# The row maximum of attention scores in two reductions, and new order tables, in a transformer block on one NeuronCore

## The chip, the cores and the metric

The kernel runs on one core of a Trainium2 chip. The metric is the device time of one execution in microseconds; the kernel before took 999.41 us as the median of three runs (999.37 to 1000.24). All data are float32. TensorE (PE) multiplies, VectorE (DVE), ScalarE (ACT) and GpSimd (POOL) work on its results, SyncE (SP) issues most of the DMAs. PE writes its products into PSUM banks of 128 partitions by 512 float32 numbers.

## The reference

One block with adaptive layer norms: sliding-window attention with 32 heads of 20, then an MLP applied to each token. There are 2048 tokens of width 640, a window of 256, and an MLP width of 1536.

```python
mod = (_silu(c) @ w_mod).reshape(c.shape[0], 6, 1, -1)
sa, ca, ga, sb, cb, gb = (mod[:, 0], ..., mod[:, 5])
h = _layernorm(x) * (1 + ca) + sa
x = x + ga * _A_ref(h, A_wqkv, A_wo)      # q, k, v; scores * 20 ** -0.5 with
                                          # 0 <= i - j < 256; softmax; @ v; @ wo
h = _layernorm(x) * (1 + cb) + sb
x = x + gb * _B_ref(h, B_w1, B_b1, B_w2, B_b2)   # layernorm, @ w1 + b1, gelu, @ w2 + b2
```

## The kernel before, in words

**Precision.** Each large product is made three times, of operands split into a high and a low part: `hhi x whi`, `hlo x whi` and `hhi x wlo`. The low parts are made by DVE or POOL (`hlo`, `wlo`, `stage`), as tables say (`LOV`, `LOWP`, `HIA`).

**Stages.** In the start (until 48.8 us of the profile), the first 1024 tokens are normalized, the modulation is worked out from `c`, and the first columns of q and k are projected, in an order written out by hand (`ORDER`, after `RUN0` warm-up products that only keep PE at work). Attention follows, to 556.5 us, then its tail to 596.9 us, then the MLP, in four blocks of 512 tokens.

**The attention loop** (`for t in range(n + LAG + PVLAG + 4)`, lines 1302 to 1351) has 128 score items: two halves of the tokens, eight quads of four heads, eight blocks of 128 queries. Item `t` computes its scores twice. First they are computed with queries on the partitions, for the row maxima only (`s_batch`, the tile `s`). Eleven iterations later (`LAG`), they come with keys on the partitions (`e_batch`, the tile `e`), with the negated maximum fed in through two more rows of the operand. An iteration does, in this order on PE: the products of `e` for item t − 11 and of `s` for item t, interleaved (`score_batch`); the products of the probabilities with v of an earlier item (`pv_stage`, tile `o`); then products that a plan puts there (`plan[t, h]`) as filling: projections of later columns (`pp`, with `pp_late` and `ppo` of the same kind), transposes (`psx`, `pv`, `pm`, `xt`, `yt`), the attention's output product (`wo`), and the sums that spread a modulation vector over all rows (`pmr`). How many `pp` products an iteration gets is set by `EXTRA`, one number for each `t`; where other steps land is set by further tables. On DVE an iteration does the mask of `e`, the mask of `s`, the maximum of `s` over the keys (`s_max`, the tile `nm`) and then planned steps: statistics of layer norms, low parts, sums. ACT takes the exp (`pt`), copies `o` out (`oT`), and makes high parts. In every eighth iteration of the first half (t = 18, 26, 34, 42, ...) there is no `e` item, so PE has only `s` products, and the filling.

**Banks.** Of `s` and `e` there is one buffer each. From t = 11 on, the 4 heads of `s` (384 keys each) share 3 banks: in slots 0 to 3, at columns 0, 384, 768 and 1152, so that slots 0 and 1 lie in banks 0 and 1, slots 2 and 3 in banks 1 and 2. Two heads are multiplied in one half of the array's rows, the other two in the other, side by side. The next products of `s` can start when the reduction of the item before has read the tile. Those of `e` can start when its exp has. The order of the products in a batch is a list:

```python
ONE = "0a 0d 0b 0e 0c 0f".split()
BOTH = ['0f', '0c', '0d', '1a', '1b', '1d', '0b', '1e', '0a', '0e', '1c', '1f']
```

The digit says whether it is of the first (`e`) or second (`s`) of the batch; with `ONE` there is only one of the two. The letters a, b and c are products of slots 0 and 1 (a in bank 1, b and c in bank 0), d, e and f those of slots 3 and 2 (d and e in bank 2, f in bank 1).

**The tail** (t from 128 on, the first iterations at 556.5 us) has no `s` any more: `e`, `o`, the output products `wo` of the fourth block of tokens, its second layer norm (`sta`, `xb`, `y`, `stb`), and its transposes `yt`, which the MLP's first products need. `WARM` puts warm-up products at places of it, `CROSS` says how much of this block's work falls into the tail, `SUMS_LAST` in which iterations ACT takes the exp before it copies `o`.

Every instruction is recorded through a helper, so all stand at line 119 in the profile of before (121 in the changed kernel), and are told apart by the names of their tiles.

Of the kernel before, what the change touches and what calls it, by code (L numbers as in the profile page):

```python
# [9 lines left out]
F32 = mybir.dt.float32  # L10
# [3 lines left out]
ALU = mybir.AluOpType  # L14
AX = mybir.AxisListType
PSUM = bass.MemoryType.PSUM

P = 128
# [14 lines left out]
RUN0 = 37  # L33
# [4 lines left out]
ORDER = ('T00 M1 L00 S0 S1 S2 R3 S3 T01 R12 L01 P00 N M2 T02 P01 M3 R3 T03 T10 L03 L02 T11 M4 R1 C L10 P02 T04 R6 P10 L11 T12 L04 P03 L12 T13 L13 P11 P04 E0 T14 Y00 P12 P13 L14 Y01 P14')  # L38
LOWP = ['L10', 'L03', 'L00', 'L14', 'L13', 'L12']


UNITS = ((0, 'q1', 'k1', 'v0', 'v1', 'q2', 'k2', 'v2', 'q3', 'k3', 'v30', 'q40', 'k40', 'v40', 'k41', 'q41', 'v41', 'v31'), (1, 'q10', 'k00', 'k10', 'q00', 'q01', 'k01', 'q11', 'k11', 'v1', 'v0', 'q2', 'k2', 'k3', 'q3', 'v2', 'v3', 'q4', 'k4', 'v4'))
FAST = 10
LNS = [-11.0, -3.5, -1.25, -1.5, 1.25, -1.0, -0.25]
LOV = [0, 1, 3, 4, 5, 6, 7, 12, 14, 17, 18, 19, 21, 23, 25, 26, 29, 40, 41, 42, 43, 46, 49, 50, 53, 56, 58, 60]
HIA = [0, 2, 6, 7, 9]
MV = [9, 12, 15, 19, 20, 21, 23, 26, 27]
# [4 lines left out]
V_COST = 2.84  # L52
# [5 lines left out]
EXTRA = {9: -2, 10: -4, 11: 7, 12: 1, 13: -2, 14: -2, 16: -2, 18: -3, 20: -5, 21: 4, 22: 6, 23: 3, 24: 1, 25: 4, 26: -1, 27: 5, 28: -4, 29: 3, 30: -3, 31: -3, 33: 4, 34: -3, 35: 2, 36: 3, 37: 3, 38: -6, 40: -2, 41: -5, 42: -3, 44: -7, 46: 2, 50: 1, 51: 1, 52: -8, 53: 7, 54: -10, 55: 1, 56: -6, 57: 3, 59: 8, 60: -2, 61: -1, 63: -1, 64: -1, 65: 2, 66: -8, 67: -2, 68: -2, 69: -2, 70: -1, 71: 3, 72: 6, 73: 3, 75: -1, 76: -2, 77: -3, 78: -2, 79: -3, 80: -3, 81: -9, 82: 19, 83: 6, 84: -2, 85: -1, 86: 2, 88: 3, 90: 2, 91: 1, 92: 3, 93: -6, 94: -11, 96: 8, 97: 1, 98: -1, 99: 5, 101: 3, 102: 1, 103: 6, 104: -4, 105: -2, 106: -1, 107: -2, 108: 3, 110: 3, 111: 6, 112: -1, 114: -1}  # L58

EARLY = {3: (5, 0, 0), 5: (3, 0, 0), 6: (3, 0, 0), 7: (3, 0, 0), 9: (5, 0, 0), 12: (1, 0, 0), 13: (0, 0, 0), 14: (0, 0, 0), 15: (5, 0, 0), 16: (5, 0, 0), 17: (4, 0, 0), 19: (4, 0, 0), 24: (4, 0, 0), 30: (5, 0, 0), 32: (0, 0, 0), 33: (3, 0, 0), 35: (5, 0, 0), 37: (5, 0, 0), 39: (5, 0, 0), 40: (4, 0, 0), 41: (3, 0, 0), 42: (4, 0, 0), 43: (2, 0, 0), 44: (2, 0, 0), 45: (0, 0, 0), 47: (5, 0, 0)}  # L60

AFTER = {0: 1, 2: 2, 3: 2, 4: 3, 5: 1, 6: 1, 7: 1, 9: 1, 10: 2, 11: 1, 12: 2, 14: 1, 15: 1, 19: 1, 20: 1, 22: 1, 23: 2, 25: 1, 32: 1, 35: 1, 36: 3, 38: 3, 40: 1, 41: 3, 42: 2, 43: 3}

SUMS_LAST = [13, 14, 18, 25, 31, 42, 46, 50, 52, 55, 58, 60, 61, 62, 63, 64, 75, 76, 77, 78, 79, 88, 90, 91, 95, 99, 101, 103, 108, 109, 110, 111, 115, 116, 117, 120, 122, 126, 127, 131, 132, 133, 136, 139]
LEAST = 4
MOST = 10
MODS = [[10.0, 17.0], [17.75, 27.5], [69.5, 79.25]]
WOS = [88.5, 91.75, 98.75, 110.25, 112.0, 113.25, 116.0]
W1S = [115.0, 122.0, 133.75]
RS = [[81.75, 82.5], [82.5, 88.75]]  # L70
TOMID = 110
WARM = {(130, 1): 3}
LATE_AT = [110.25, 110.5, 110.75, 111.5, 113.75, 114.0, 116.5]
TAIL0 = [115.25, 120.25, 124.25, 129.0]
NEXT = 134.0
CROSS = 0.72
LO0 = 4.6
PER = 4.821
LATE = 0.8152
TAIL_AT = {'rd': -1.372, 'ri': -1.024, 'load': -0.924, 'om': -0.246, 'oh': 0.058, 'ol': 0.133, 'w00': 0.287, 'w01': 0.36, 'w02': 0.382, 'w03': 0.416, 'w04': 0.511, 'add0': 0.569, 'sa0': 0.649, 'w10': 0.71, 'w11': 0.711, 'w12': 0.722, 'w13': 0.855, 'w14': 0.865, 'add1': 0.885, 'sa1': 1.178, 'n1': 1.2, 'm0': 1.327, 'x0': 1.343, 'x1': 1.544, 'm1': 1.344, 'sb0': 1.505, 'sb1': 1.557, 'n2': 1.683, 'y0': 1.844, 'y0l': 1.922, 'y1': 2.026, 'y1l': 2.38}  # L80
# [44 lines left out]
def block_kernel(ctx: ExitStack, tc: tile.TileContext, x, wqkv, wo, w1, b1, w2, b2, c, crow, wmod, wcol, sel, outT):  # L125
# [425 lines left out]
    def score_batch(batches):  # L551
# [51 lines left out]
    def s_max(it, s, c0):  # L603
# [3 lines left out]
        nc.vector.tensor_reduce(it["quad"]["nm"][:, :, it["key"][2]], s[:, :, max(c0, P) : 384], AX.X, ALU.max)  # L607
# [878 lines left out]
```

## Time and profile before

| what | us |
|---|---|
| median of 3 runs (lowest, highest) | 999.41 (999.37, 1000.24) |
| the profiled execution | 1000.15 |
| its span, from the first instruction to the last | 998.4 |
| PE, DVE, ACT, POOL busy | 955.0, 593.0, 443.1, 479.4 |
| mean granted clock of PE, as a share of full speed | 0.988 |
| the stages' ends: start, attention, tail, MLP | 48.8, 556.5, 596.9, 985.0 |

A row of the profile gives line, engine, operation, tiles (out<-in), shapes, how often, then the busy time in us and the mean of one in ns, then the idle time ahead and the instruction whose end ended it. A timeline row gives start and duration in us, the instruction, how many follow each other (a matmul of full float32 shows as two records), and in brackets the idle time ahead with the releaser. The iteration numbers `t` are counted from the `s` batches.

### The profile page before, as it was taken

Reading aid. Unit: us, or ns where it says so; the run is one execution under the profiler, and the core shown is the slowest. Engines: PE = TensorE matmul, PEld = TensorE weight load, DVE = VectorE, ACT = ScalarE, POOL = GpSimd, SP = SyncE. Lnnn points to the kernel's source line nnn. Section 1 sums busy time; section 2 is a strip of 40 time slices with the busy share of each in tenths; the row PEclk is TensorE's granted clock in tenths of the full one; section 3 lists DMA queues with packets and bytes.
Section 4 is the critical chain, followed back from the end, with each engine's and each line's share of the span. In section 5 each row is a group of like instructions: output and inputs, shape, how many; then the busy total and the mean of one; then the engine's idle time right before and its main releaser. Section 6 shows DMA issues by size and latency. Waiting matters only on the chain.

```text
span 998.4 us, 19991 instructions
## 1 busy us (share of the span) xinstructions
PE 955.0 (96%) x7745; PEld 753.3 (75%) x7745; DVE 593.0 (59%) x938; ACT 443.1 (44%) x777; POOL 479.4 (48%) x671
## 2 busy tenths in 40 slices
PE   8899999999999999999998879999999999999997
PEld 8777677666777777777676667888888888888886
DVE  6664868878766787767678656565444443333112
ACT  3724545566655544554445664333432343333122
POOL 4324555576764254544536855654543444442221
PEclk9999999999999999999699999999999999999999
DMA  8364877637768368834672235344422344124113
GB/s 301 105 217 140 273 241 257 195 106 211 227 198 254 91 198 258 245 110 152 198 190 64 78 95 188 125 122 137 135 85 85 103 126 123 41 66 145 53 44 115
DMA packets 98974, 152.17 MB, mean 152 GB/s; under 512 B 8864, under 2 KB 42112, under 8 KB 98880
## 3 DMA queue, kind: packets, MB, share of 16 engines
q1 hardware_dynamic: 89664, 142.50, 46.9%
q10 hardware_dynamic: 9216, 8.39, 2.7%
q8 instruction: 62, 1.02, 0.4%
q14 instruction: 32, 0.26, 0.1%
HBM read 98.51 MB, written 51.58 MB: 150 GB/s over the span
## 4 chain that ended last, share of the span: by engine, by line
PE 78%; DVE 10%; ACT 5%; issue 3%; POOL 2%; DMA 2%; DVEq 0%; ACTq 0%; POOLq 0%
PE pp L119 16%; PE out L119 16%; PE h L119 15%; PE e L119 7%; PE o L119 6%; PE wo L119 6%; PE s L119 5%; DVE e L119 4%; ACT pt L119 3%; DVE nm L119 2%; PE ppo L119 2%; PE warm L119 1%; DVE s L119 1%; PE yt L119 1%; DMA w2r<-in_w 1%
## 5 line engine op out<-in xcount | busy, mean ns | idle before, releaser
L119 POOL TENSOR_SCALAR_AFFINE_SELECT pt<-pt 128x512 f32<-128x512 f32 x192 | 129.1, 672 | 151.9 <-ACT pt L119 145.3
L119 ACT ACTIVATE pt<-e 128x1024 f32<-128x1024 f32 (+1 forms) x120 | 133.6, 1113 | 69.4 <-DVE e L119 66.4
L119 POOL TENSOR_TENSOR w2lo<-w2r,w2hi 128x640 fp32r<-128x640 f32 x48 | 77.3, 1609 | 169.8 <-ACT w2hi L119 169.4
L119 DVE TENSOR_REDUCE nm<-s 128x4 f32<-128x1024 f32 (+1 forms) x128 | 152.7, 1193 | 4.4
L119 PE MATMUL e<-qbuf,kbuf 62*128 62x128 f32 (+2 forms) x773 | 114.4, 332 | 15.3 <-ACT pt L119 14.4
L119 PEld LDWEIGHTS e<-qbuf,kbuf 62*128 62x128 f32 x773 | 79.0, 189 | 56.0 <-ACT pt L119 31.9
L119 PE MATMUL s<-kbuf,qbuf 60*128 60x256 f32 (+2 forms) x728 | 106.8, 311 | 9.4 <-DVE nm L119 6.7
L119 PE MATMUL pp<-hhi,whi 128*128 128x512 f32 x265 | 114.7, 433 | 0.3 <-ACT pf L119 0.2
L119 DVE CAST ghi<-g 128x512 fp32r<-128x512 f32 x48 | 27.4, 571 | 144.7 <-ACT g L119 144.6
L119 DVE COPY_PREDICATED e<-mask_t,e 128x512 f32<-128x512 uint32 x96 | 66.6, 694 | 76.5 <-PE e L119 71.7
L119 PE MATMUL pp<-hlo,whi 128*128 128x512 f32 x265 | 107.9, 407 | 1.3 <-DVE hlo L119 1.3
L119 PE MATMUL pp<-hhi,wlo 128*128 128x512 f32 x265 | 108.6, 410 | 0.4 <-POOL wlo L119 0.4
L119 PE MATMUL o<-pt,vbuf 128*32 128x128 f32 x2688 | 101.6, 281 | 0.3 <-ACT vbuf L119 0.2
L119 PEld LDWEIGHTS s<-kbuf,qbuf 60*128 60x128 f32 x728 | 81.9, 190 | 22.6 <-DVE nm L119 6.1
L119 PE MATMUL out<-ghi,w2hi 128*128 128x512 f32 x240 | 96.0, 400 | 0.0
L119 PE MATMUL h<-yhi,w1hi 128*128 128x512 f32 x240 | 95.9, 399 | 0.0
L119 PE MATMUL out<-ghi,w2lo 128*128 128x512 f32 x240 | 93.9, 391 | 0.0
L119 PE MATMUL out<-glo,w2hi 128*128 128x512 f32 x240 | 93.8, 391 | 0.0
L119 PE MATMUL h<-yhi,w1lo 128*128 128x512 f32 x240 | 93.8, 391 | 0.0
L119 PE MATMUL h<-ylo,w1hi 128*128 128x512 f32 x240 | 93.8, 391 | 0.0
L119 POOL TENSOR_TENSOR wlo<-wraw,whi 128x128 fp32r<-128x128 f32 x170 | 73.6, 464 | 38.7 <-ACT whi L119 37.3
L119 ACT COPY oT<-o 128x128 f32<-128x128 f32 x128 | 33.8, 264 | 128.8 <-PE o L119 119.0
(169 smaller groups left out, 1842.9 us busy)
## 6 DMA issues: line engine op xcount, KB each, us to landing
w2r<-in_w SPq DMA_DIRECT2D x48, 320.0 KB
qbuf<-q_scr SPq DMA_DIRECT2D x60, 240.0 KB
wraw<-in_wqkv SPq DMA_DIRECT2D x35, 320.0 KB
kbuf<-k_scr SPq DMA_DIRECT2D x44, 240.0 KB
q_scr<-stage SPq DMA_DIRECT2D x20, 512.0 KB
k_scr<-stage SPq DMA_DIRECT2D x20, 512.0 KB
o_scr<-oT ACTq DMA_DIRECT2D x64, 128.0 KB
wm<-in_wmod SPq DMA_DIRECT2D x20, 320.0 KB
```

Of the source, the lines that this page charges most:

```text
L119: return self.tc.keep_in_program_order(op(*args, **kw))
```

## The change

The maximum of `s` is taken by two instructions, one for slots 0 to 2 and one for slot 3, except in the 18 iterations of `WHOLE` and where the tile is 512 wide. For each, the banks it reads are noted; a product of the next item in a bank that a reduction does not read is declared free of it. So products in banks 0 and 1 wait for the first reduction alone, those in bank 2 for both. All `s` tiles of 384 become one tile for this. There are 99 iterations with two reductions.

```diff
+    fixed, maxima = {}, []
+
     def score_banks(kind, name):
         n = width()
-        t = pools[kind].tile([P, 4 * n], F32, tag=kind, name=name)
+        if kind == "s" and n == 384:
+            if "s" not in fixed:
+                fixed["s"] = pools[kind].tile([P, 4 * n], F32, tag=kind, name=name)
+            t = fixed["s"]
+        else:
+            t = pools[kind].tile([P, 4 * n], F32, tag=kind, name=name)
...
             ins = matmul(out, lhs, rhs, start=True, stop=True).ins
+            if n == len(batches) - 1 and width() == 384:
+                for red, banks in maxima:
+                    if bank not in banks:
+                        tc.declare_no_dep(ins, red, reason="no bank of the maximum")
...
-        nc.vector.tensor_reduce(it["quad"]["nm"][:, :, it["key"][2]], s[:, :, max(c0, P) : 384], AX.X, ALU.max)
+        del maxima[:]
+        n = width()
+        for lo, hi in ((0, CUT), (CUT, 4)) if n == 384 and now[0] not in WHOLE else ((0, 4),):
+            red = nc.vector.tensor_reduce(
+                it["quad"]["nm"][:, lo:hi, it["key"][2]], s[:, lo:hi, max(c0, P) : 384], AX.X, ALU.max
+            )
+            if n == 384:
+                maxima.append((red.ins, range(lo * n // 512, (hi * n - 1) // 512 + 1)))
```

The tables have new numbers throughout. The ones that the text speaks of:

```diff
-RUN0 = 37
+RUN0 = 35
...
+CUT = 3
+WHOLE = [12, 26, 28, 29, 39, 44, 47, 48, 55, 63, 68, 85, 108, 109, 111, 116, 118, 127]
...
-WARM = {(130, 1): 3}
+WARM = {(127, 2): 4, (130, 1): 2, (135, 0): 6, (136, 0): 4, (141, 1): 2}
...
-CROSS = 0.72
+CROSS = 1.07
```

Of `EXTRA`, t = 12, 32 and 33 go from 1, none and 4 to −2, −3 and 2; `SUMS_LAST` has 44 entries before and 46 now, 30 of them the same; `ORDER`, `LOV`, `LOWP` and `HIA` send four low parts of stages from DVE to POOL and three `hlo` the other way. The counts of all other products stay as they were. Where the rows move, for three places:

PE in iterations t33 (ending with its filling) and the first product of t34, which has only `s` products. `o` are the probabilities' products, `pp` the projections. Before:

```order
L119 MATMUL o_2_4_2166<-pt_2_4_2060,vbuf_104 32x128 x4
L119 MATMUL pp_1_4_2116<-hlo_251,whi_2024 128x512
L119 MATMUL pp_1_4_2116<-hhi_250,wlo_2025 128x512
L119 MATMUL pp_1_4_2116<-hhi_250,whi_2024 128x512
L119 MATMUL pp_1_4_2116<-hlo_251,whi_2024 128x512
L119 MATMUL pp_1_4_2116<-hhi_250,wlo_2025 128x512
L119 MATMUL s_4_2_2209<-kbuf_100,qbuf_97 128x256
```

and in the changed kernel:

```order
L121 MATMUL o_2_4_2152<-pt_2_4_2049,vbuf_104 32x128 x4
L121 MATMUL pp_0_4_2106<-hlo_249,whi_2014 128x512
L121 MATMUL pp_0_4_2106<-hhi_248,wlo_2015 128x512
L121 MATMUL pp_0_4_2106<-hhi_248,whi_2014 128x512
L121 MATMUL pp_0_4_2106<-hlo_249,whi_2014 128x512
L121 MATMUL pp_0_4_2106<-hhi_248,wlo_2015 128x512
L121 MATMUL pmr_1_2178<-acc_1596,ones 128x320
L121 MATMUL pp_0_4_2106<-hhi_248,whi_2014 128x512
L121 MATMUL pp_0_4_2106<-hlo_249,whi_2014 128x512
L121 MATMUL pp_0_4_2106<-hhi_248,wlo_2015 128x512
L121 MATMUL s_1_3_995<-kbuf_100,qbuf_97 128x256
```

Three `pp` products have come here from t32 and the row sum `pmr` from t29.

DVE at the same place: the two masks of `e`, the mask of `s` and its maximum, and the layer norm's statistics (`st`, `mv`). Before:

```order
L119 COPY_PREDICATED e_2_6_2146<-mask_t,negc 128x4x128 x2
L119 COPY_PREDICATED s_4_1_2147<-mask_t,negc 128x4x128
L119 TENSOR_REDUCE nm_4_2082<-s_4_1_2147 128x4
L119 BN_STATS st_2139<-xt_1_1766 128x6 x2
L119 BN_AGGR mv_2140<-st_2139 128x2
```

and now:

```order
L121 COPY_PREDICATED e_2_6_2133<-mask_t,negc 128x4x128 x2
L121 COPY_PREDICATED s_1_3_995<-mask_t,negc 128x4x128
L121 TENSOR_REDUCE nm_4_2072<-s_1_3_995 128x3
L121 TENSOR_REDUCE nm_4_2072<-s_1_3_995 128x1
L121 BN_STATS st_2126<-xt_1_1799 128x6 x2
L121 BN_AGGR mv_2127<-st_2126 128x2
```

Nothing else has moved there; the second reduction stands directly behind the first.

PE in the tail, iterations t135 to t137 (`yt` transposes the fourth block's normalized rows). Before:

```order
L119 MATMUL o_7_1_7679<-pt_7_2_7614,vbuf_102 32x128 x4
L119 MATMUL yt_3_7697<-idn,y_7491 128x128 x2
L119 MATMUL e_7_5_7707<-qbuf_96,kbuf_99 128x384 x4
L119 MATMUL o_7_2_7713<-pt_7_3_7655,vbuf_102 32x128 x4
L119 MATMUL e_7_6_7743<-qbuf_96,kbuf_99 128x384 x4
```

and now:

```order
L121 MATMUL o_7_1_7671<-pt_7_2_7606,vbuf_102 32x128 x4
L121 MATMUL warm_0_7689<-idn 128x128 x6
L121 MATMUL yt_3_7696<-idn,y_7483 128x128 x2
L121 MATMUL e_7_5_7706<-qbuf_96,kbuf_99 128x384 x4
L121 MATMUL o_7_2_7712<-pt_7_3_7646,vbuf_102 32x128 x4
L121 MATMUL warm_0_7731<-idn 128x128 x4
L121 MATMUL e_7_6_7747<-qbuf_96,kbuf_99 128x384 x4
```

Ten warm-up products stand ahead of the exp scores of two items. Two more follow the last `yt`, ahead of the MLP's first product. Nine products `wo` that stood among the MLP's first ones stand in the tail instead, three of them ahead of the last exp scores and six behind those, between the products `o` that follow. On DVE the statistics of the second norm and the sum of the residual (`xb`) change places in t138. Before:

```order
L119 COPY_PREDICATED e_7_7_7789<-mask_t,negc 128x4x128 x2
L119 BN_STATS stb_7820<-y_7741 128x6 x2
L119 BN_AGGR mvb_7827<-stb_7820 128x2
L119 TENSOR_SCALAR rsb_7828<-mvb_7827 128x1
L119 TENSOR_TENSOR xb_7574<-wo_0_7778,xb_7574 128x320
```

and now:

```order
L121 BN_STATS stb_7792<-y_7745 128x6
L121 COPY_PREDICATED e_7_7_7798<-mask_t,negc 128x4x128 x2
L121 TENSOR_TENSOR xb_7568<-wo_0_7782,xb_7568 128x320
L121 BN_STATS stb_7792<-y_7745 128x6
L121 BN_AGGR mvb_7835<-stb_7792 128x2
```

One half of the statistics now stands ahead of the masks, the other behind the sum.

More of the change, by code (lines that the diff above doesn't have):

```diff
@@ L50 @@
 LAST = 108
-V_COST = 2.84
+V_COST = 2.87
 X_COST = 1.79
@@ L71 @@
+WOS = [88.75, 91.75, 98.75, 110.25, 112.0, 112.25, 116.0]
+W1S = [115.25, 121.0, 134.25]
+RS = [[81.0, 82.0], [83.0, 88.25]]
 TOMID = 110
-WARM = {(130, 1): 3}
-LATE_AT = [110.25, 110.5, 110.75, 111.5, 113.75, 114.0, 116.5]
+WARM = {(127, 2): 4, (130, 1): 2, (135, 0): 6, (136, 0): 4, (141, 1): 2}
+LATE_AT = [110.25, 110.5, 110.75, 111.0, 113.75, 114.25, 116.75]
 TAIL0 = [115.25, 120.25, 124.25, 129.0]
-NEXT = 134.0
-CROSS = 0.72
-LO0 = 4.6
+NEXT = 133.85
+CROSS = 1.07
+LO0 = 4.5
 PER = 4.821
-LATE = 0.8152
```

30 lines of the change are left out of this document (14 added, 16 removed).

## The prediction

> **What bounds the kernel now.** I read the page first (busy shares and granted clock), then busy time by stage, then the list of waits, then the timeline at the longest stalls. From the head of the page:
>
> ```profile
> span 998.4 us, 19991 instructions
> PE 955.0 (96%) x7745; PEld 753.3 (75%) x7745; DVE 593.0 (59%) x938; ACT 443.1 (44%) x777; POOL 479.4 (48%) x671
> PEclk9999999999999999999699999999999999999999
> ```
>
> TensorE is busy for 955.0 of 998.4 us. All that any reordering can win is the 43.4 us in which it is idle, and the time in which it runs at a lower clock: one slice near 490 us shows a 6. The stages say where the idle time lies; the columns are the stretch, its length, the busy time of PE, PEld, DVE, ACT and POOL, and the granted clock, DMA share and rate:
>
> ```profile
> 0.00:48.80 48.80, 43.68 (x272) 39.22 (x272) 31.09 (x109) 26.90 (x39) 20.02 (x32) 0.97 0.58 202
> 97.40:474.20 376.80, 364.25 (x3992) 268.18 (x3991) 285.16 (x363) 201.06 (x378) 206.64 (x339) 1.00 0.67 202
> 474.20:556.50 82.30, 73.37 (x871) 55.44 (x871) 64.03 (x89) 40.42 (x72) 45.50 (x59) 0.90 0.53 143
> 556.50:596.90 40.40, 32.26 (x483) 23.99 (x482) 23.06 (x49) 24.55 (x43) 27.15 (x43) 1.00 0.26 74
> 596.90:985.00 388.10, 386.04 (x1876) 325.45 (x1875) 159.12 (x290) 130.72 (x206) 166.49 (x172) 1.00 0.35 108
> ```
>
> The MLP (596.9 to 985) has 2.1 us of idle TensorE: nothing is to be had there except by taking products out of it. Attention proper has 12.6, its thin end 8.9, the tail behind the last maximum 8.1, the start 5.1. VectorE, which makes the maxima, is busy for 285 of 376.8 us in attention, so it has a quarter of its time free. From the waits (who <- for whom: us, times, longest):
>
> ```profile
> PE e L119 <- ACT pt L119: 14.4, 24, 1.6
> PE s L119 <- DVE nm L119: 6.7, 13, 1.4
> DVE e L119 <- PE e L119: 88.7, 80, 2.3
> ```
>
> The wait that the title is about, products of maximum scores behind the reduction `nm`, is 6.7 us in 13 places: that is the ceiling of the split by itself. The exps cost twice that, and the split doesn't touch them. In the other iterations VectorE itself waits for TensorE (80 times): there the reduction is done before its banks are asked for.
>
> **The split.** The reductions, and an independent instruction that follows them, by shape:
>
> ```profile
> L119 DVE TENSOR_REDUCE nm<-s 128x4 f32<-128x1024 f32 x120 | 147.1, 1226 | 4.1
> L119 DVE TENSOR_REDUCE nm<-s 128x4 f32<-128x512 f32 x8 | 5.5, 692 | 0.3
> ```
>
> A line through the two gives 1.04 ns an element (534 ns for 512) and 158 ns fixed. Three heads (768) should take 0.96 us, one head (256) 0.43. The place with the longest stall, iteration t34 that has no exp item (first PE, then DVE; start, duration, what, and in brackets the idle time ahead and its releaser):
>
> ```profile
> 183.06 0.86 PE L119 MATMUL o<-pt,vbuf 128*32 128x128 f32 x24
> 184.90 0.40 PE L119 MATMUL pp<-hhi,wlo 128*128 128x512 f32 x1
> 186.71 0.86 PE L119 MATMUL s<-kbuf,qbuf 60*128 60x256 f32 x6 [1.41 <-DVE nm L119]
> ```
>
> ```profile
> 184.56 0.74 DVE L119 COPY_PREDICATED_SCALAR s<-mask_t,negc 128x512 f32 x1
> 185.34 1.23 DVE L119 TENSOR_REDUCE nm<-s 128x4 f32<-128x1024 f32 x1
> 186.48 0.88 DVE L119 BATCH_NORM_STATS2 st<-xt 128x6 f32<-128x320 f32 x2
> ```
>
> The statistics start 0.09 before the reduction ends, so an independent successor hides 0.09 of its fixed part: the second piece should add 0.158 − 0.09 = 0.07 us. The first then frees banks 0 and 1 about 0.27 earlier (0.96 against 1.23), the second frees bank 2 0.07 later. Which counts? In the order of products, the second or third one of a batch lies in bank 2 and in the other row half, and it used to run beside the first. TensorE issues in order: when this product waits for the second piece, all behind it wait too. What runs early is one or two products of some 0.29 us (six in 0.86, two at a time), and the row half of bank 2, which sets the batch's end, starts 0.07 later. So a stalled batch gains nothing, between −0.1 and +0.07. For the price I take the 13 stalls and the 24 exp stalls behind which VectorE is pressed: 37 × 0.07 at most 2.6, most of it under the 88.7 us in which VectorE waits for TensorE; **+0.5 us**. The ends: 0, if all is hidden, and 37 × 0.158 = 5.8, if nothing overlaps and the fixed part is paid at each. VectorE's own time rises by 99 × 0.07 = 7 us (15.6 without overlap), out of the 92 us it has idle in attention.
>
> [...]
>
> **What the tables move into the longest stall.** As the order shows, three projection products go from iteration t32 to t33, and one row sum `pmr` from t29 to t33, in front of the maximum scores of t34. The sizes come from the group of pmr (two records a product), from a row of the pp products, and the place they leave from the stretches of t29 and t32:
>
> ```profile
> L119 PE MATMUL pmr<-acc,ones 128*128 128x320 f32 x12 | 4.2, 431 | 0.0
> 167.50:171.50 4.00, 4.00 (x37) 2.97 (x39) 2.52 (x3) 2.56 (x5) 3.29 (x7) 1.00 1.00 259
> 178.50:182.00 3.50, 3.50 (x39) 2.47 (x37) 3.39 (x7) 1.71 (x4) 3.21 (x8) 1.00 0.62 230
> 184.19 0.40 PE L119 MATMUL pp<-hhi,wlo 128*128 128x512 f32 x1
> ```
>
> From 184.19 to 184.90 three pp products pass, 0.24 each. 3 × 0.24 + 4.2/6 = 1.4 us of work fills a stall of 1.41. With pmr go ScalarE's copy out of its bank, which it shares with the sums `o` (the next of them starts only behind the s products of t34), and one store on SP's queue, whose rows are read some sixty iterations later: both at nothing. Where it came from, TensorE had no gap (4.00 of 4.00, 3.50 of 3.50), so those iterations become shorter by the same: **−1.4 us** (at worst 0: VectorE's masks, freed no sooner, would then end t29 and t32). The stall has a second price, in the granted clock just behind it:
>
> ```profile
> 185.06:188.47 3.41, 2.00 (x33) 1.38 (x32) 3.31 (x8) 2.78 (x5) 1.59 (x4) 1.00 0.25 98
> 188.47:191.89 3.42, 3.42 (x13) 2.38 (x13) 3.10 (x7) 0.22 (x1) 1.90 (x4) 0.50 0.71 249
> 215.78:219.19 3.41, 2.06 (x23) 1.48 (x24) 3.04 (x5) 2.61 (x4) 0.34 (x1) 1.00 0.02 5
> ```
>
> A window with 2.00 us of work is followed by 3.42 us at half clock, in which TensorE is busy throughout. At full clock that work is 1.71 shorter. Filled, the window before it has 3.3 us of work and the clock should stay up: **−1.4 us**, a little under the full 1.71, since VectorE and ScalarE set part of the next iteration; the ends are 0 and −1.71.
>
> The Trainium skill, page "TensorE: Matmul & The Clock Gate", section "Why this matters for your kernels", asks only that no gap exceed about 3 us, since it takes an idle window to halve the clock. By it a 1.41 us stall costs no clock, and this term would be 0 and the sum 1.4 higher. The trace decides against it: 0.50 stands right behind that stall.
>
> **The tail.** There the tables add warm-up products (4, 6, 4 and 2 at t127, t135, t136 and t141, one less at t130) and take nine products `wo` out of the MLP's side into it. The rows:
>
> ```profile
> 581.42 0.62 PE L119 MATMUL e<-qbuf,kbuf 62*128 62x384 f32 x4 [1.21 <-ACT pt L119]
> 583.89 0.62 PE L119 MATMUL e<-qbuf,kbuf 62*128 62x384 f32 x4 [1.05 <-ACT pt L119]
> 588.78 0.68 PE L119 MATMUL e<-qbuf,kbuf 62*128 62x256 f32 x8 [1.58 <-ACT pt L119]
> 593.10 0.41 PE L119 MATMUL wo<-wo_hhi,ot 128*128 128x320 f32 x1 [0.86 <-DVE xb L119]
> 593.50 0.46 PE L119 MATMUL wo<-wo_hhi,ot 128*128 128x320 f32 x2
> 593.79 0.31 PE L119 MATMUL wo<-wo_hlo,ot 128*128 128x320 f32 x1
> 596.68 0.44 PE L119 MATMUL yt<-idn,y 128*128 128x128 f32 x2 [0.37 <-DVE ylo L119]
> ...
> 16.43 2.84 PE L119 MATMUL warm<-idn 128*128 128x128 f32 x24
> 19.03 0.47 PE L119 MATMUL pp<-hhi,whi 128*128 128x512 f32 x1
> ```
>
> Twelve warm-ups (two records each) take 2.60 us from start to start, 0.22 each. Six in the 1.21 stall are 1.3: +0.1. Four in the 1.05 stall: 0. Two behind the last transposes, ahead of the MLP's first product: that one waits for nothing in the trace, so they cost their full 0.4. Four at t127, where the exp scores start without a stall:
>
> ```profile
> 556.51 0.62 PE L119 MATMUL e<-qbuf,kbuf 62*128 62x384 f32 x4
> 557.94 0.70 DVE L119 COPY_PREDICATED e<-mask_t,e 128x512 f32<-128x512 uint32 x1
> ```
>
> These scores end at 557.13 and VectorE masks them only at 557.94, so 0.81 of 0.88 is hidden: +0.1. Nine products `wo` at 0.147 (593.50 to 593.79 for two) are 1.3 us that leave the MLP's first products, a place without gaps, and run in stalls of 1.58, 0.86 and 0.37: −1.3. That also needs the second statistics on VectorE to stand behind the sum `xb`, as the order shows. The tail is −1.3 + 0.1 + 0.1 + 0.4, **−0.7 us**; the ends are +2.0 (none of the 15 added warm-ups, 3.3 us, is hidden, against the −1.3) and −2.2 (the 0.86 stall goes as a whole).
>
> The rest I put at **0**, ±0.5: in the start, the same transposes, products and low parts stand in another order and the last warm-ups fall from 37 to 35, but the waits there hang on the modulation; four low parts more go to POOL and ScalarE, off the path; single products move by one iteration.
>
> **The sum**, against the profiled execution's own 1000.15 (span 998.4 and 1.75 around it): 1000.15 − 1.4 − 1.4 + 0.5 − 0.7 = 997.15. The median of the runs stands 0.74 below the profiled execution: **996.4**.
>
> **Rivals.**
> *The lower clock moves to the next stall.* The stall at t42 is 1.35 us, and its window had 2.06 us of work against 2.00: just above the edge. Nothing is added in front of it, the second piece makes it 0.07 longer, and everything arrives nearly 3 us earlier while the windows seem to keep their 3.41 grid. If 2.0 is the edge, it now halves the clock: +1.4, so 997.8. With the tail's gain lost too, up to 999. For it: the two windows differ by 0.06. Against: the first product of the batch now starts earlier and puts work into the window. Or the half clock behind t34 had another cause than the stall and simply stays: the same 1.4 and 997.8, as the window at t42, with nearly the same stall, had no such end. By the Trainium skill's page "TensorE: Matmul & The Clock Gate", weighed above, it would. Chance of the two together 0.25, all of it within 0.2% of before.
> *The second piece is paid in full (slower).* Place: the s products in iterations where VectorE is late. Price: 158 ns in each of 37, 5.8 instead of 0.5: 996.4 + 5.3 = 1001.7, and more if batches that were not stalled now are. It decides once the end of the second piece falls behind TensorE's arrival, that is where VectorE does not wait for the exp scores first. For it: VectorE is busy for 64 of 82 us in the thin end. Against: 88.7 us of waiting in 80 iterations. Chance 0.2.
> *The long stretch at half clock shrinks.* Near 490 us the clock is at 0.50 for five windows, begun by stalls in iterations without fill:
>
> ```profile
> 478.60:482.00 3.40, 3.18 (x36) 2.06 (x35) 2.52 (x3) 1.19 (x2) 1.05 (x3) 0.50 0.95 237
> ```
>
> If an earlier arrival splits those stalls over two windows, each window that is spared saves at most 1.6 (half of 3.18), in an iteration that VectorE and ScalarE nearly fill rather 0.7: five give −3.5, 992.9. For it: the phase moves by about 3 us. Against: several stalls follow each other there, and nothing is filled. Chance 0.1.
> *The split doesn't do what it says*, and the products of the free banks start no earlier, as worked out above for all but one or two of a batch: the +0.5 says so already, and without any cost of it the time is 995.9, inside the forecast.
>
> **How the numbers follow.** Forecast 996.4, between 994.7 and 997.4: 0.45. Rivals 0.25, 0.2, 0.1. Two tenths of a per cent, 2 us, is about what a measurement of this kernel can tell from no change: faster means under 997.4, slower over 1001.4. Faster 0.45 + 0.1 = 0.55; same 0.25 and a little of the slower rival, 0.27; slower 0.18. The range goes from the shrunk stretch to the paid second piece, 992.9 to 1001.8, which leaves out some 0.15.
>
> **What would show it.** In the profile after: the stall ahead of the s products of t34 under 0.3 us and a granted clock of 1.00 in all windows from 100 to 470 us; reductions of 0.96 and 0.43 us, the second starting just before the first ends; the waits of s for `nm` near 5 us (6.7 less the 1.4); stalls of 0 to 0.3 at the two warmed places of the tail, and the MLP beginning with nine products `wo` fewer. Wrong would be a 0.50 window behind t42, more waits of s for `nm` than 13, or exps that start later against their iteration in the tail.

## The result, and the profile after

The changed kernel takes **990.45 us** (median of 5 runs, 989.71 to 991.24) against 1000.24 for the kernel before beside it (5 runs, 999.37 to 1001.88): the ratio is 0.990, 95% interval 0.9886 to 0.9915. The forecast was 996.4, in a range from 992.9 to 1001.8; 990.45 lies under that range. The direction was right; of the 9.8 us it had 3.0 (997.15 against the profiled execution, 996.4 as a median).

The head of the page after:

```profile
span 989.3 us, 20081 instructions
PE 954.7 (97%) x7769; PEld 756.2 (76%) x7769; DVE 597.9 (60%) x1035; ACT 444.6 (45%) x782; POOL 481.0 (49%) x672
```

TensorE's busy time is that of before (954.7 against 955.0): of the 9.1 us that the span lost 8.8 are idle time, 34.6 us of it now instead of 43.4. VectorE has 4.9 us more, less than the 7 that were forecast for the second pieces. The same stretches as before (they now begin and end some us further on in the program):

```profile
97.40:474.20 376.80, 366.71 (x4066) 272.02 (x4064) 293.13 (x450) 205.63 (x386) 213.35 (x346) 1.00 0.67 205
474.20:556.50 82.30, 73.25 (x895) 56.60 (x898) 62.81 (x103) 41.91 (x76) 49.49 (x66) 0.91 0.43 127
556.50:596.90 40.40, 36.76 (x460) 28.87 (x449) 22.70 (x49) 23.86 (x40) 23.47 (x37) 1.00 0.35 115
```

The thin end of attention still has its half clock (0.91 in the second row). The waits that were quoted of before:

```profile
PE e L121 <- ACT pt L121: 11.4, 21, 1.3
PE s L121 <- DVE nm L121: 2.3, 5, 1.1
DVE e L121 <- PE e L121: 78.5, 80, 2.2
```

The waits of `s` for `nm` fell from 6.7 us in 13 places to 2.3 in 5, where "near 5" was forecast. Where the time went along the program, from the starts of the iterations in the two traces: 0.25 us ahead of t0 and 7.1 more up to t107 (2.1 of it from the start of t29 to that of t35); 0.2 is given back in the thin end and 0.5 among the warm-ups of the tail; 1.4 is won between the last exp scores and the third block of the MLP; another 1.0 lies behind the last product, where the last output lands (the span ends 5.5 us after that product's start in the one trace, 4.5 in the other). That last 1.0 isn't clearly the change's: the end takes 4.5 us in eleven of the sixteen traces of this study and 5.2 to 6.3 in the other five, one of which is a version of the changed kernel.

The stall that the first two terms were about, in front of the s products of t34 (PE, then DVE):

```profile
182.75 0.70 PE L121 MATMUL pmr<-acc,ones 128*128 128x320 f32 x2
184.08 0.91 PE L121 MATMUL s<-kbuf,qbuf 60*128 60x256 f32 x6
```

```profile
182.97 1.29 DVE L121 TENSOR_REDUCE nm<-s 128x3 f32<-128x768 f32 x2
184.18 0.88 DVE L121 BATCH_NORM_STATS2 st<-xt 128x6 f32<-128x320 f32 x2
```

It is filled: no idle time in brackets. The pieces, by shape:

```profile
L121 DVE TENSOR_REDUCE nm<-s 128x3 f32<-128x768 f32 x94 | 90.1, 959 | 3.2
L121 DVE TENSOR_REDUCE nm<-s 128x1 f32<-128x256 f32 x94 | 39.0, 415 | 0.0
```

0.96 and 0.415 us, as the line through the two old shapes had it (0.96 and 0.43), and the pair of them takes 1.29, 0.06 more than the one reduction. So the instructions cost what they should. What was wrong is what the products do with it.

### The profile page after: what moved, and what is told of

Read it like the earlier page. It is cut to its first block, busy times and chain, and to the rows that moved or that the text cites. A ratio compares the mean times of both kernels' runs of the same rounds, so it can differ in the third digit from the quotient of the medians.

```text
span 989.3 us, 20081 instructions
## 1 busy us (share of the span) xinstructions
PE 954.7 (97%) x7769; PEld 756.2 (76%) x7769; DVE 597.9 (60%) x1035; ACT 444.6 (45%) x782; POOL 481.0 (49%) x672
## 3 DMA queue, kind: packets, MB, share of 16 engines
q8 instruction: 62, 1.02, 0.4%
## 4 chain that ended last, share of the span: by engine, by line
PE 80%; DVE 8%; ACT 4%; DMA 3%; POOL 2%; issue 2%; SPq 0%; DVEq 0%; ACTq 0%; POOLq 0%
PE pp L121 17%; PE h L121 16%; PE out L121 16%; PE e L121 7%; PE o L121 7%; PE wo L121 6%; PE s L121 4%; ACT pt L121 3%; DVE e L121 3%; PE ppo L121 2%; PE warm L121 1%; PE yt L121 1%; POOL pt L121 1%; DVE nm L121 1%; PE xt L121 1%
## 5 line engine op out<-in xcount | busy, mean ns | idle before, releaser
L121 DVE TENSOR_REDUCE nm<-s 128x1 f32<-128x256 f32 (+4 forms) x227 | 159.0, 737 | 4.4
L121 PEld LDWEIGHTS e<-qbuf,kbuf 62*128 62x128 f32 x773 | 82.7, 188 | 52.0 <-ACT pt L121 27.9
L121 PE MATMUL s<-kbuf,qbuf 60*128 60x384 f32 (+2 forms) x728 | 109.3, 307 | 4.9 <-DVE nm L121 2.3
L121 PEld LDWEIGHTS s<-kbuf,qbuf 60*128 60x128 f32 x728 | 91.2, 189 | 15.6 <-DVE nm L121 6.6
L121 DVE COPY_PREDICATED s<-mask_t,s 128x512 f32<-128x512 uint32 x112 | 77.2, 689 | 14.5 <-PE s L121 14.5
```

The costliest lines, as they stand in the source:

```text
L121: return self.tc.keep_in_program_order(op(*args, **kw))
```

## The experiments

Each is compared with the kernel before, run beside it on the same chip (its medians lie between 1000.2 and 1000.8, its single runs between 997.9 and 1002.5). Theory A at the outset: the split itself brings what was missed, because the products of the two row halves take turns. Theory B: it brings nothing, and the moved steps bring all.

**The tables without the split.** The list of iterations left whole takes in all:

```diff
-WHOLE = [12, 26, 28, 29, 39, 44, 47, 48, 55, 63, 68, 85, 108, 109, 111, 116, 118, 127]
+WHOLE = range(128)
```

> The changed kernel with every maximum in one instruction (the tables, the one s tile and all else as changed). Theory A, the split itself brings what the forecast missed, since the s products of the two row halves take turns, and each product that starts early makes its batch shorter: some 0.15 us at each late reduction, 4 to 5 us in all, so 994.5 to 995.5. Theory B, the split brings nothing, as the prediction had it, and the moved steps bring all: 990 to 990.5.

Measured: 994.08 us, ratio 0.9937 (0.992 to 0.9953). That is a little under theory A's 994.5 to 995.5. Without the split, 3.6 us of the 9.8 are gone. Theory B falls.

**The split without the tables.** The kernel before with the changed `score_banks`, `score_batch` and `s_max` of the diff above, `CUT` and `WHOLE` as there, and no other number changed.

> The kernel before with the split alone (its tables, the same list of iterations left whole). Theory A: 4 to 5 us under the kernel before, 995 to 996, the waits of s for nm falling from 6.7 to under 4 us, and batches of the seven iterations with only s ending 0.15 us earlier against their reduction. Theory B: the time of before or 0.5 above, 1000 to 1001.

Measured: 993.31 us, ratio 0.9928 (0.9911 to 0.9944), and 3.4 us of waits of s for nm in 6 places. It is more than theory A had asked for, and 7.2 with 6.4 of the tables make 13.6 where the two together give 9.8. Something is in both. The single tile of `s` is, and both shorten the stall of t34, which is 1.05 us here instead of 1.41.

**Two reductions, and every product waiting for both.** The lines that release a product are out:

```diff
             ins = matmul(out, lhs, rhs, start=True, stop=True).ins
-            if n == len(batches) - 1 and width() == 384:
-                for red, banks in maxima:
-                    if bank not in banks:
-                        tc.declare_no_dep(ins, red, reason="no bank of the maximum")
```

> The changed kernel with the two reductions, but every s product waiting for both: it shows the price of the second instruction. Theory A: slower than the version with one reduction by up to 99 x 0.07 us where it shows, 995 to 999. Theory B, that the end of a batch hangs on the product behind the second piece anyway: within 1 us of the changed kernel, 990.5 to 991.5.

Measured: 995.99 us, ratio 0.9959 (0.9941 to 0.9977): 1.9 over the version with one reduction, 5.5 over the changed kernel. In t42, from the reduction's start to the products `o` behind the batch (PE, then DVE):

```profile
215.65 0.88 PE L121 MATMUL s<-kbuf,qbuf 60*128 60x256 f32 x6 [1.40 <-DVE nm L121]
216.47 0.32 PE L121 MATMUL o<-pt,vbuf 128*32 128x128 f32 x4
```

```profile
214.31 1.29 DVE L121 TENSOR_REDUCE nm<-s 128x3 f32<-128x768 f32 x2
```

216.47 − 214.31 = 2.16; with one reduction it is 2.09. The second piece costs 0.07 us a time, the size that the prediction had worked out, and it is the release that turns it into a gain.

**The single tile alone.** The split's code on the kernel before, with the list of the whole iterations taking in all:

```diff
-WHOLE = [12, 26, 28, 29, 39, 44, 47, 48, 55, 63, 68, 85, 108, 109, 111, 116, 118, 127]
+WHOLE = range(128)
```

> The kernel before with the one s tile for all items of 384 and nothing else of the change: each maximum in one instruction, its tables. It tells whether the single tile, which the versions with and without the split share, has a part in what they gain. If the split alone is the cause of split_only's 7 us: the time of before, 999.5 to 1001. If the overlap of the two halves of the change (7.2 + 6.4 against 10.0 together) is the tile's: 996.5 to 997.5.

Measured: 998.02 us, ratio 0.9973 (0.9961 to 0.9986; single runs from 995.7 to 999.9). It lies between the two expectations: 2.2 us. The prediction hadn't priced this edit at all. What it does can be read from the eight iterations with s products alone. In the kernel before, the first product of the batch waits for DVE alone in four of them, and for DVE and for an earlier product of PE in the other four, as the order of its waits shows (in 65 of the 117 iterations on tiles of 384 it waits for both). From the reduction's start to `o` it is 2.09 to 2.10 us in the first four and 2.16 in the others. With the single tile the second wait is gone, and it is 2.09 in all eight. One of the other four is t58, in the kernel before:

```profile
278.34 1.23 DVE L119 TENSOR_REDUCE nm<-s 128x4 f32<-128x1024 f32 x1
280.50 0.32 PE L119 MATMUL o<-pt,vbuf 128*32 128x128 f32 x4
```

and with the single tile:

```profile
276.75 1.23 DVE L121 TENSOR_REDUCE nm<-s 128x4 f32<-128x1024 f32 x1
278.84 0.32 PE L121 MATMUL o<-pt,vbuf 128*32 128x128 f32 x4
```

That this wait is all that the single tile brings is not shown: the stall of t34 is 1.32 us here instead of 1.41, and this trace has no half clock behind it.

**What the moved steps of t33 are worth.** The changed kernel with three pp products back in t32 and pmr back in t29:

```diff
-EXTRA = {..., 32: -3, 33: 2, ...}
+EXTRA = {..., 32: 0, 33: -1, ...}
...
-AFTER = {..., 21: 3, ...}
+AFTER = {...}
```

> The changed kernel with three pp products back from t33 in t32 and the row sum pmr back in t29, all else as changed. The prediction's step: 1.4 us for the stall and 1.4 for the half clock behind it, 993.3. With the split in place the stall is some 0.27 shorter, 1.1 us, and its window holds 2.3 us of work instead of 2.0: if the amount of work in the window decides, no half clock comes back and the time is 991.3 to 991.8; if any stall over 1 us does it, it comes back.

Measured: 992.79 us, ratio 0.9921 (0.9906 to 0.9936), 2.3 over the changed kernel and above the 991.3 to 991.8 that were expected without a half clock. By the trace, the iterations t29 to t35 (to the start of t36) are 1.7 us longer. The stall ahead of t34 is back:

```profile
186.07 1.00 PE L121 MATMUL s<-kbuf,qbuf 60*128 60x256 f32 x6 [1.05 <-DVE nm L121]
169.34 0.81 PE L121 MATMUL pmr<-acc,ones 128*128 128x320 f32 x2 [0.70 <-ACT oT L121]
```

1.05 instead of 1.41, and no half clock stands behind it. The second row says that the undoing isn't quite clean: in t29 the row sum now waits 0.70 us for ScalarE to free its bank, since the changed tables let the exp go first there.

**Do the row halves take turns?** The kernel before, with the products of a batch of s alone issued one row half after the other:

```diff
-ONE = "0a 0d 0b 0e 0c 0f".split()
+ONE = "0a 0b 0c 0d 0e 0f".split()
```

> The kernel before with the products of an iteration that has only s (or only e) products issued one row half after the other (a b c d e f instead of a d b e c f). Theory A, the two row halves take turns on something they share: the batches of t34 and t42 stay at 0.79 to 0.85 us, and the time at 1000 to 1001. Theory B, they run side by side: those batches take 1.2 us or more, 20 such batches cost 0.3 to 0.4 us each where TensorE is the bound, 1004 to 1008.

Measured: 999.44 us, ratio 0.999 (0.9981 to 1.0), and those batches last 0.78 to 0.82 us as before. That looked like theory A. But in the trace the product d, now fourth in the queue, still starts 0.01 us after a: it passes b and c, which are of a's row half and start 0.22 and 0.28 us after a.

**Bank 2 last.** The changed kernel, with an order that lets four of six products go before the second reduction:

```diff
-ONE = "0a 0d 0b 0e 0c 0f".split()
-BOTH = ['0f', '0c', '0d', '1a', '1b', '1d', '0b', '1e', '0a', '0e', '1c', '1f']
+ONE = "0a 0b 0c 0f 0d 0e".split()
+BOTH = ['0f', '0c', '0d', '1a', '1b', '0b', '1c', '0a', '0e', '1f', '1d', '1e']
```

> The changed kernel with the products of bank 2 issued last in both orders (a b c f d e), so that two thirds of a batch wait for the first reduction alone. Theory A: the 0.33 us between the two pieces is covered by products instead of holding up the queue, another 0.05 to 0.1 us at each late reduction, 988.5 to 990. Theory B: the row halves no longer run side by side, 0.2 us or more in each of 117 batches, 1010 and up.

Measured: 1003.31 us, ratio 1.0028 (1.0016 to 1.004), 12.9 over the changed kernel, between the two expectations. The shortest batch of both kinds with twelve products lasts 1.19 us instead of 1.02. If only the sum counted, the order could not cost 0.17. Theory A falls too. A third one fits all of it. **Theory C:** bank 1 is written by both row halves, first by a, then by f, and f waits until a is done. So the batch ends with a, then f, and it was f that set its end, not the product behind the last reduction. With d and e put behind f, those come on top. The wait is the kernel's own: where a product writes a bank after one of the other row half, `score_batch` puts a no-op ahead of it that waits for that one (in the kernel before, the trace of t42 has a semaphore wait of 0.05 us in TensorE's queue there, 0.04 us after the end of a).

**A late, and b and c early.** Two orders for s alone, one on the kernel before, one on the changed kernel:

```diff
-ONE = "0a 0d 0b 0e 0c 0f".split()
+ONE = "0c 0a 0b 0d 0e 0f".split()
```

> The kernel before with the order c a b d e f in iterations that have only s products: a, the product that gives bank 1 over to f of the other row half, starts behind c (384 columns) instead of first. Theory C, a batch ends with f, which starts 0.53 us after a since it waits for a to be done with bank 1: batches of t34 and t42 grow by the 0.2 to 0.3 us that a starts later, from 0.79-0.81 to 1.0-1.1. Theory A, the row halves share a rate and only the sum counts: 0.81 as before. Beside it, whether the window at half clock behind the 1.41 us stall of t34 is there in this execution too (its loop up to there is that of before).

```diff
-ONE = "0a 0d 0b 0e 0c 0f".split()
+ONE = "0a 0b 0c 0d 0e 0f".split()
```

> The changed kernel with the order a b c d e f in iterations that have only s products, so that a, b and c go at the first reduction's end and only d, e and f stand behind the second. Theory C, there the end of the batch hangs on d, e, f of the second half: from the start of the first reduction to the products o 1.94 us, as in the changed kernel. Theory A: b and c done early shorten it too, to 1.75 to 1.85.

One execution each is timed, at 1005.5 and 989.41 us. The batch of t42 with a late, all six products, then f and `o`:

```profile
218.53 1.06 PE L119 MATMUL s<-kbuf,qbuf 60*128 60x384 f32 x6 [1.35 <-DVE nm L119]
...
219.23 0.35 PE L119 MATMUL s<-kbuf,qbuf 60*128 60x256 f32 x1
...
219.52 0.44 PE L119 MATMUL o<-pt,vbuf 128*32 128x128 f32 x4
```

0.99 us instead of 0.81, with f 0.70 after the batch's start: a bit under the 1.0 to 1.1 expected, and far from theory A's 0.81. With b and c ahead of the second reduction (the changed kernel otherwise):

```profile
214.28 1.00 PE L121 MATMUL s<-kbuf,qbuf 60*128 60x256 f32 x6 [1.07 <-DVE nm L121]
215.20 0.32 PE L121 MATMUL o<-pt,vbuf 128*32 128x128 f32 x4
```

```profile
213.26 1.29 DVE L121 TENSOR_REDUCE nm<-s 128x3 f32<-128x768 f32 x2
```

215.20 − 213.26 = 1.94, as in the changed kernel without it, where theory A asked for 1.75 to 1.85. Both are theory C's.

**The warm-up products.** The changed kernel with the three of before, in two sets of runs, with none at all, and in the second set once more unaltered beside them:

```diff
-WARM = {(127, 2): 4, (130, 1): 2, (135, 0): 6, (136, 0): 4, (141, 1): 2}
+WARM = {(130, 1): 3}
```

> The changed kernel with the warm-up products of before (three at t130, none at t127, t135, t136 and t141). By the prediction's step the added ones cost 0.6 us and hold up nothing: 989.9. Rival: they keep the clock up in the tail, and without them a window at half clock stands there: 991.5 to 993.

> The changed kernel unaltered, so that the versions beside it are compared on one chip: 990 to 991.

> The changed kernel with the warm-up products of before, once more beside the changed kernel. If the added warm-ups are a cost (0.9 us at t127, 0.4 ahead of the MLP by the two traces): 1.3 to 1.8 us under the changed kernel. If the first comparison was chance: no difference.

> The changed kernel without any warm-up product in attention and its tail. If warm-ups there are only a cost: the time of the version with the three of before, or 0.2 us less. If those three hold the clock up behind t130: a window at half clock in the tail and 1 us more.

Measured: 988.62 us, ratio 0.9877 (0.9861 to 0.9894), in the first set; in the second 988.25, ratio 0.9891 (0.9874 to 0.9907), beside 989.69, ratio 0.9901 (0.9887 to 0.9914), for the changed kernel unaltered (a little under its own 990 to 991). None at all: 990.01, ratio 0.9903 (0.9888 to 0.9917). With the old three, the first trace has 1.4 us less from the first warmed place to the last product; the medians say 1.4 to 1.8. It is the fastest version of the study, though the intervals overlap. The rival has something for it, too. Without any, two stretches of the tail run at half clock, behind stretches with 2.0 us of work in 3.6 and 1.9 in 3.3:

```profile
555.00:558.60 3.60, 2.02 (x31) 1.33 (x25) 2.33 (x6) 2.46 (x4) 3.37 (x6) 1.00 0.49 146
558.60:562.00 3.40, 3.40 (x37) 2.82 (x36) 2.27 (x4) 2.30 (x3) 2.28 (x4) 0.53 0.33 100
572.50:575.80 3.30, 1.94 (x38) 1.09 (x30) 1.95 (x5) 2.35 (x5) 3.05 (x5) 1.00 0.12 40
575.80:579.20 3.40, 2.50 (x29) 1.61 (x30) 1.25 (x4) 1.01 (x2) 3.24 (x5) 0.51 0.00 0
```

In the second set the version with the old three had one such stretch as well, in the first none; the two traces of the changed kernel have none in the tail. So the added warm-ups seem to hold the clock, and by the medians they cost more than it is worth.

**Two reductions everywhere.** The list of iterations left whole is empty:

```diff
-WHOLE = [12, 26, 28, 29, 39, 44, 47, 48, 55, 63, 68, 85, 108, 109, 111, 116, 118, 127]
+WHOLE = []
```

> The changed kernel with two reductions in all 117 iterations, the 18 of the list too. If the second piece costs its 0.07 us only where VectorE is late, and brings 0.05 to 0.15 where TensorE waits: within 0.7 us of the changed kernel. If the list keeps it off the path of the exps: 2 us more, with longer waits of e for pt.

Measured: 991.64 us, ratio 0.9922 (0.9909 to 0.9936), 1.9 over the changed kernel beside it. The waits of e for pt are not longer (12.6 us in 20 places against 12.8 in 21), so the time is that of the second expectation, without the longer waits that were to go with it. The two profiled executions differ by 3.4 us: 1.7 of it lie behind the last product, in the end that changes from trace to trace, 1.1 from t110 to t114, in the thin end of attention, and 0.7 from t11 to t107. Where the list helps stays open.

## Why the prediction was right in its sign and wrong in its size

**Its own time in the changed kernel, term by term.** The forecast was −1.4 (stall), −1.4 (clock), +0.5 (split), −0.7 (tail). The three of the tables make −3.5, and the tables brought 3.9 us on top of the single tile (998.02 to 994.08) and 2.9 on top of single tile and split (993.31 to 990.45). The sum of these three was right, in part by luck: the half clock is not in what the tables brought there, since neither the trace of the single tile nor that of tile and split has a window behind t34, and the tail brought more than its 0.7 (both below). The miss is the split, which brought 3.6 (994.08 to 990.45) to 4.7 (998.02 to 993.31) where it was to cost 0.5, and the single tile, 2.2, which was not priced. These two are the difference between the forecast's 3.0 and the measured 9.8.

**The step that failed** reads: "when this product waits for the second piece, all behind it wait too", and from it, "the row half of bank 2, which sets the batch's end, starts 0.07 later. So a stalled batch gains nothing, between −0.1 and +0.07." The waiting in order is right. What failed is "which sets the batch's end": bank 2 did not set it. The two batches of t42, first the kernel before: a, f and the products behind the batch, and the reduction:

```profile
218.13 0.38 PE L119 MATMUL s<-kbuf,qbuf 60*128 60x256 f32 x1 [1.35 <-DVE nm L119]
218.66 0.35 PE L119 MATMUL s<-kbuf,qbuf 60*128 60x256 f32 x1
218.94 0.32 PE L119 MATMUL o<-pt,vbuf 128*32 128x128 f32 x4
```

```profile
216.85 1.23 DVE L119 TENSOR_REDUCE nm<-s 128x4 f32<-128x1024 f32 x1
```

and the changed kernel, with d and b between a and f:

```profile
214.06 0.38 PE L121 MATMUL s<-kbuf,qbuf 60*128 60x256 f32 x1 [1.07 <-DVE nm L121]
214.39 0.44 PE L121 MATMUL s<-kbuf,qbuf 60*128 60x384 f32 x2
214.72 0.33 PE L121 MATMUL s<-kbuf,qbuf 60*128 60x256 f32 x1
214.98 0.32 PE L121 MATMUL o<-pt,vbuf 128*32 128x128 f32 x4
```

```profile
213.04 1.29 DVE L121 TENSOR_REDUCE nm<-s 128x3 f32<-128x768 f32 x2
```

(the second row of the changed kernel is d and b, which start together once the second piece is done). In the kernel before, f starts 0.53 us after a, and `o` 0.28 after f: the batch ends with bank 1 handed from a to f. In the changed kernel f starts 0.34 after d, so where it starts 0.53 after both a and d, d had 0.19 us to spare. Measured from the reduction's start, a now starts 0.27 earlier and d 0.07 later, and the slack of d is what is won: 218.94 − 216.85 = 2.09 us from reduction to `o` before, 214.98 − 213.04 = 1.94 after. So a stalled batch gains 0.15, and 0.22 where the second wait of the first product went too. The experiments with a late, with b and c early, and with bank 2 last show that it is a and then f, and with the split d's half, that set the end: 0.99 us for the batch in the first, 1.94 and 2.00 (218.75 − 216.76, in t42) from reduction to `o` in the other two. No run takes the no-op between a and f away, so what a batch would last without it is open.

**The size of the stage was misread too.** "The ceiling of the split by itself", 6.7 us in 13 places, was the idle time that the list of waits shows. In an iteration with both kinds, the s products wait among e products, TensorE never stands still for the list, and the batch lasts longer. Of the 82 batches of both kinds from t19 to t107, 61 have twelve products, and the shortest of these lasts 1.02 us; in the kernel before 27 of them last more than 1.06, and the 61 lie 6.4 us above 1.02 in all; in the changed kernel it is 18 and 4.2. (The others have 10, 14 or 15 matmul records, and the shortest of each take 0.81, 1.00 and 1.16.) One of the 61, t81 (with the start of the batch of t80 as the first row, and the mask of `e` and the reduction of t80), in the kernel before:

```profile
362.00 0.56 PE L119 MATMUL e<-qbuf,kbuf 62*128 62x256 f32 x3
365.50 0.56 PE L119 MATMUL e<-qbuf,kbuf 62*128 62x256 f32 x3
366.01 0.44 PE L119 MATMUL s<-kbuf,qbuf 60*128 60x256 f32 x3
366.83 0.32 PE L119 MATMUL o<-pt,vbuf 128*32 128x128 f32 x4
```

```profile
363.41 0.69 DVE L119 COPY_PREDICATED e<-mask_t,e 128x512 f32<-128x512 uint32 x1
364.73 1.23 DVE L119 TENSOR_REDUCE nm<-s 128x4 f32<-128x1024 f32 x1
```

and in the changed kernel:

```profile
355.73 0.56 PE L121 MATMUL e<-qbuf,kbuf 62*128 62x256 f32 x3
359.01 0.56 PE L121 MATMUL e<-qbuf,kbuf 62*128 62x256 f32 x3
360.13 0.32 PE L121 MATMUL o<-pt,vbuf 128*32 128x128 f32 x4
```

```profile
356.75 0.69 DVE L121 COPY_PREDICATED e<-mask_t,e 128x512 f32<-128x512 uint32 x1 [1.21 <-PE e L121]
358.08 1.29 DVE L121 TENSOR_REDUCE nm<-s 128x3 f32<-128x768 f32 x2
```

The batch lasts 1.34 before (365.50 to 366.83), with no idle time in brackets, and 1.12 after. And the wait feeds itself: with s products late in t80, the e products queued behind them are late, so VectorE masks `e` 1.41 us after the batch's start (363.41 − 362.00) instead of 1.02, the reduction comes later against the next batch, and that waits again. A row such as "VectorE waits for TensorE 80 times" was taken as slack of the reduction; part of it was this loop.

**What the loop gained, by the traces.** From the first product of t11's batch to the `o` behind that of t107 the kernel before takes 373.5 us, the version with the single tile 370.9, that with tile and split 368.7, the changed kernel 366.4. Of the first step of 2.6, some 1.1 is the half clock behind t34, which of these four only the trace of before has. So the tile brings 1.5, the split 2.2, the tables 2.3. The split's 2.2 is found in its batches: 1.0 in the seven of s alone that have two reductions, and 1.4 in the 61 of twelve products (5.8 to 4.4 us above 1.02). The medians give the split 4.7 on that kernel. Of the rest, 1.5 is that the profiled execution with the single tile ran so far under its median (996.48 against 998.02), and 1.1 lies in the end behind the last product. Neither is shown to be the split's.

**The stall at t34**: right. t33_all puts 1.7 us on the steps moved into t33, where 1.4 was forecast. The wait of pmr, 0.70, is in it, which leaves some 1.0 for the stall itself; the split alone had already cut it to 1.05.

**The half clock behind it**: right that it hangs on the stall, as far as the traces show (there is none behind t34 where the stall is filled or cut to 1.05), wrong as a sure gain of the change. Its price is 1.13 us. The iteration t34 in the kernel before, and in the version one_serial, which up to there differs only in the order within the batches of s alone and has the same stall:

```profile
186.71:191.00 4.29, 4.29 (x36) 2.83 (x36) 4.19 (x10) 1.34 (x4) 3.35 (x6) 0.71 0.42 153
```

```profile
186.51 0.85 PE L119 MATMUL s<-kbuf,qbuf 60*128 60x256 f32 x6 [1.41 <-DVE nm L119]
186.51:189.67 3.16, 3.16 (x36) 2.21 (x36) 3.06 (x8) 1.35 (x4) 2.99 (x6) 1.00 0.52 193
```

4.29 us with the window, 3.16 without, at the same stall of 1.41. In a_late it was there again. So it differs from one execution to the next; that it hangs on how the stall falls into the 3.41 us windows fits, but is only argued. The median of before then holds only part of it, and a term taken from one profiled execution was set in full.

**The tail**: right in sign, too small. From the last maximum to the last product the trace has 0.9 less where 0.7 was forecast, but this pair is at the low end: from the start of t127 to the first product of the MLP's third block, four traces with the tail of before (before, one_serial, fixed_only, split_only) take 254.8 to 255.8 us (a_late, with a half-clock window in the MLP, is left out) and eight with the changed one 252.6 to 254.2, 1.8 less in the mean. The warm-ups cost 1.4 rather than 0.6 (against warm_old, the four at t127 delayed `e` by 0.94, of which the next iterations returned half), so all else that changed there, the moved wo products above all, brings well over the forecast 1.3.

**The rivals.** "The second piece is paid in full": no, 0.07 each, and 1.9 us in all without the release. "The lower clock moves to the next stall": it can; with the tables alone a window at half clock stands behind t42 (216.8 to 220.2), and in a_late behind both, but not in the changed kernel, whose stall there is 1.07. "The long stretch at half clock shrinks": in the changed kernel's first profile it is five windows as before (471 to 488.5), in the second, after_again, one (483 to 486.5), with the same tables. So it can, by execution. Its price is not shown: from t110 to t114 the two take 19.62 and 18.84 us, 0.8 apart where 3.5 was forecast, but after_serial, with four windows there, takes 18.02.

## What to carry to other kernels

A wait inside an interleaved batch doesn't show as idle time: compare the length of the batch with that of the shortest with the same products, over all iterations, before a ceiling is read off a list of waits. To say which product ends a batch, follow each hand-over of a bank and each engine half to the end, with its own start in the trace; the one released last need not be the one that ends it, and a wait that the kernel itself sets between two products can be the longer chain. And a clock window behind a stall is a lottery ticket, to be priced by its chance, not as a sure term.

## What the runs showed of the hardware

A product that waits for two engines' semaphores started later than one that waits for one: 2.16 against 2.09 us from the reduction's start to the end of the batch, in eight of eight places, and 2.09 in all with the second wait gone. The trace has a semaphore instruction of 0.05 us of its own for the first of the two waits. The edit that takes the second wait away brought 2.2 us (998.02); how much of that is the wait alone isn't separated.

A product of one row half of the array can start ahead of two of the other half that stand before it in the queue (one_serial: d 0.01 us after a, b and c 0.22 and 0.28 after it). A product that waits for a semaphore does hold up what is behind it: b started 0.33 after a, with d, in the changed kernel, and 0.22 after it where it stood ahead of d.

The stretches at half clock inside the traces last 3.41 us or two, four or five times that, and where they begin differs from execution to execution. The same stall of 1.41 us had one behind it in two traces of three. How little work brings one on isn't settled here by TensorE's busy time: in tables_only 2.07 us in a window was followed by half clock, in the kernel before 1.94 was not:

```profile
213.35:216.76 3.41, 2.07 (x35) 1.42 (x33) 3.04 (x5) 2.38 (x3) 0.98 (x1) 1.00 0.04 10
216.76:220.17 3.41, 3.41 (x10) 2.73 (x11) 1.52 (x2) 0.82 (x2) 1.55 (x4) 0.50 0.25 43
```

```profile
581.01:584.42 3.41, 1.94 (x32) 1.19 (x32) 1.87 (x5) 2.43 (x5) 3.16 (x5) 1.00 0.12 38
584.42:587.84 3.42, 2.78 (x39) 2.30 (x37) 0.85 (x2) 1.11 (x3) 2.04 (x5) 1.00 0.02 5
```

So the edge at 2.0 us that the prediction weighed is not a rule. The Trainium skill, page "TensorE: Matmul & The Clock Gate", section "Part 1: The HAM clock gate (the "warmup" mystery)", says that the window of 3413 ns runs freely and doesn't reset when a kernel starts; the traces agree with the length and with the changing phase. Its section "Why this matters for your kernels" has the clock fall only after an idle window, a gap of about 3 us; here a gap of 1.41 was enough in two traces of three, so the measurement decides.
